# A windowed attention and token mixing kernel: its hand written order of work and its evictions arranged anew

## The chip, the cores and the metric

The kernel runs on one core of a Trainium2 chip. A core has five engines that run side by side, each through its own list of instructions: PE multiplies matrices, DVE and ACT do elementwise work and move results out of PSUM, POOL and SP are used here mainly to issue DMAs. [...] The metric is the device time of one execution in microseconds (us); lower is better.

## The reference

Two layers follow each other. The first is attention with a sliding window of 128 and a linear position bias (8 batches, 8 heads, 576 positions, 64 values per head); the second mixes the tokens of each batch through two small projections.

```python
# attention: q, k, v are [8, 8, 576, 64] in float32
scores = q @ k.T / 8 + bias          # bias = -slope[head] * |i - j|
scores = where((i >= j) & (i - j < 128), scores, -1e9)
attn = softmax(scores)
x = (attn @ v)  -> [8, 576, 512]     # heads side by side
# token mixing, per batch
wq, wk = x @ w_q, x @ w_k            # [576, 64]
W_tok = wq @ wk.T / 8                # [576, 576]
out = relu(W_tok @ x) @ w_out        # [8, 576, 512]
```

W_tok is never formed: the kernel computes G = wk.T x first, and then wq G.

## The kernel before

The work is cut into some 740 named operations, each with one engine. Loops at the end of the kernel create them for every batch b, with what each depends on; they do not set the order. The order is a text, `ORDER`, written out by hand at lines 35 to 117: one word for every operation, such as `QK1.3.0@PE:0`, which says the operation, its engine and the PSUM bank that it fills. Each engine gets its operations in the order in which they stand in the text. An engine never overtakes: an operation that has to wait holds up all that stands behind it on the same engine.

PSUM is held as four pairs of banks, 0 to 3. `:2` takes the whole pair 2, `:20` its first half and `:21` its second. A product can start only when the bank's last content has been moved out.

`+7` behind a bank puts seven zero products ahead of an operation: products of a tile of zeros (`fill`), whose result nobody reads. They keep PE occupied.

The operations of a batch, by name (E in front means the eviction from PSUM):

- `Lq`, `Lk`, `Lv`, `Lt`: loads of 128 rows each of q, k, v, and of the last 64 rows ("tails") of two batches. [...] `Lw`, `Lwo` load the weights. Batch 0 has loads of its own for q and k: `Lf0.0`, `Lf1.0` in float32, issued by SP, and `Lh0.1`, `Lh1.1`, issued by POOL.
- `TQ` and `ETQ`, `TT` and `ETT`: q and k are turned on PE (line 232, for batch 0 also 229), and moved to the tile `qkT` (lines 236 to 244).
- `QKb.g.u`: scores of key block g and half u of the heads; `EXP` (line 551, always ACT): the exponential to the tile `pt`; `MUL` (line 561, always DVE): times the bias and the mask as a factor.
- `PVb.t`: the product with v; `R` (line 612) and `X` (line 615), always DVE: the division by the sum, to the tile `x`. Part 4 is the tails of two batches together.
- `XT`, `EXT`: x turned; `WQ`, `EWQ`: projections to `wqk`; `EWD` (always ACT): a second copy; `WKT`, `EWK` (for the last batch `WK`): k's projection with the tokens in the partitions; `G`, `EG`: the small product to `gs`.
- `MX`, `RM` (lines 755 on ACT, 757 on DVE): the mixed tokens and relu; `OUT`, `EO` (236 on ACT, 238 on DVE): the last product, to the tile `osb`; `DO`: the store, issued by POOL (line 822, tails 825) for the batches 0 to 5, and by SP for 6 and 7. There are 26 buffers `osb` of full width, used in turn.

Before the first batch some constants are made: `iota`, `dist` and `mask` give the distances, `bias0` and `bias1` (ACT) the factors for the two halves of the heads, `biasl0` and `biasl1` copy these for the last key block; `ident` (POOL) and `idh` (DVE) are the identity for turning; `zeros`, `empty`, `ones` (DVE) and `pads` (POOL, three memsets, lines 338 to 340) set columns that no load writes. The distances lie in a part of the tile `nat` that the q rows of batch 3 take later.

Loads on POOL have `iota` ahead of them, and the stores of batches 0 to 5 stand behind all loads. Between two engines the framework adds the waits that follow from tiles; the helpers `apart` and `lone` (lines 248 and 265) take out waits between parts of one bank or tile that do not touch, for operations that hold a bank or write certain tiles, and read the list `deps` for that alone.

## Time and profile before

| | us |
|---|---|
| median of 3 runs | 135.16 |
| lowest, highest | 134.41, 135.35 |
| the profiled execution | 134.84 |
| its span, from the first to the last instruction | 132.8 |

The profile is of one execution. Some rows of it group instructions: a row of the timeline has the start, the length of a group of equal neighbours on an engine, the engine, the line, the operation, what it writes and reads, how many there are (`x4`), and in brackets how long the engine was idle before it and what ended that. A row of the groups has the number of instructions, their busy time, the mean of one in ns, and the idle time before them. PEld is the loading of weights into PE, which goes along with PE. Operations of one kind share a line, so that an operation is found by its place in the order: `ETQ1.0`, say, is the first of the two 2048-wide copies on DVE at line 244.

Most of the work by kind, in the groups of the page:

```profile
L551 ACT ACTIVATE pt<-pair 128x1024 f16<-128x1024 f32 x64 | 63.1, 1040 | 3.6 <-PE pair L229 3.1
L229 PE MATMUL pair<-wout_sb,rm 128*128 128x512 f16 (+1 forms) x132 | 31.9, 373 | 0.2 <-ACT wkn L242 0.2
L561 DVE TENSOR_TENSOR pt<-pt,bias 128x2048 f16<-128x2048 f16 x24 | 29.0, 1216 | 1.6 <-ACT pt L551 1.5
L615 DVE TENSOR_TENSOR x<-pair,inv 128x512 f16<-128x512 f32 x32 | 22.1, 690 | 0.9
```

The exponentials alone are 63.1 us of ACT.

### The profile page before, as it was taken

The page shows a single profiled execution, that of the slowest core. Times are in us where ns is not written, and L with a number is a line of the kernel's source. Part 1 is how long each engine was busy: PE and PEld are TensorE (multiplying, and loading weights), DVE is VectorE, ACT ScalarE, POOL GpSimd, SP SyncE. Part 2 cuts the span into 40 slices and gives each one's busy share as a digit, 9 for nine tenths or more (in the row PEclk, how much of TensorE's full clock was granted, in tenths as well). Part 3 has the DMA queues.
Part 4 walks back from the last instruction along what each step waited for, and adds up shares of the span by engine and source line. Part 5 has one row for each costly group of instructions (what it writes and reads, how often), then busy time and mean ns, then how long its engine had stood idle before and what let it go on. Part 6 is the DMA issues. An engine that isn't in the chain of part 4 may idle for free.

```text
span 132.8 us, 5411 instructions
## 1 busy us (share of the span) xinstructions
PE 119.8 (90%) x2360; PEld 77.9 (59%) x2360; DVE 110.1 (83%) x186; ACT 112.7 (85%) x166; POOL 109.8 (83%) x148
## 2 busy tenths in 40 slices
...
DMA  3999999999999999999999999999999729999963
GB/s 107 261 160 156 155 157 155 155 155 157 181 156 159 154 157 154 154 154 153 155 157 154 156 153 154 154 152 156 153 206 410 300 80 295 352 347 298 352 249 94
DMA packets 111431, 25.12 MB, mean 189 GB/s; under 512 B 105840, under 2 KB 108656, under 8 KB 111408
## 3 DMA queue, kind: packets, MB, share of 16 engines
...
q8 instruction: 18, 0.29, 0.8%
...
## 4 chain that ended last, share of the span: by engine, by line
PE 42%; ACT 26%; DMA 10%; POOL 7%; DVE 6%; issue 5%; POOLq 0%; ACTq 0%; DVEq 0%
PE pair L229 37%; ACT pt L551 15%; DMA nat<-in_k_dram 6%; PE pair L232 5%; DMA vt<-in_v_dram 5%; ACT qkT L242 4%; POOL nat L380 3%; POOL vt L380 3%; DVE pt L561 2%; ACT osb L236 2%; ACT rm L755 2%; ACT wqd L242 1%; DVE x L615 1%; ACT gs L236 1%; DVE wqk L238 1%
## 5 line engine op out<-in xcount | busy, mean ns | idle before, releaser
L551 ACT ACTIVATE pt<-pair 128x1024 f16<-128x1024 f32 x64 | 63.1, 1040 | 3.6 <-PE pair L229 3.1
L380 POOL DMA_DIRECT2D vt<-in_v_dram x32 | 31.4, 1136 | 1.0 <-DMA nat<-in_k_dram 0.8
L229 PE MATMUL pair<-wout_sb,rm 128*128 128x512 f16 (+1 forms) x132 | 31.9, 373 | 0.2 <-ACT wkn L242 0.2
L561 DVE TENSOR_TENSOR pt<-pt,bias 128x2048 f16<-128x2048 f16 x24 | 29.0, 1216 | 1.6 <-ACT pt L551 1.5
L380 POOL DMA_DIRECT2D nat<-in_q_dram x29 | 29.1, 1053 | 0.5 <-ACT wqd L242 0.3
L380 POOL DMA_DIRECT2D nat<-in_k_dram x29 | 28.8, 1051 | 0.1
L229 PE MATMUL pair<-qkT 64*128 64x256 f16 (+2 forms) x320 | 23.0, 250 | 2.0 <-ACT qkT L242 0.8
L229 PEld LDWEIGHTS <-pt 128*128 128x128 f16 (+1 forms) x576 | 18.8, 100 | 7.0 <-issue 2.5
L615 DVE TENSOR_TENSOR x<-pair,inv 128x512 f16<-128x512 f32 x32 | 22.1, 690 | 0.9
L229 PE MATMUL pair<-vt,pt 128*128 128x65 f16 (+1 forms) x512 | 21.6, 194 | 0.9 <-DMA vt<-in_v_dram 0.5
L822 POOL DMA_DIRECT2D out_dram<-osb x24 | 13.6, 628 | 7.5 <-DVE osb L238 5.1
L229 PEld LDWEIGHTS <-rm 128*128 128x128 f16 x132 | 11.4, 97 | 11.2 <-issue 1.2
L236 ACT COPY osb<-pair 128x512 f32<-128x512 f32 (+1 forms) x24 | 13.7, 582 | 3.7 <-PE pair L229 3.7
L229 PEld LDWEIGHTS <-qkT 64*128 64x128 f16 x320 | 11.4, 94 | 8.9 <-issue 3.5
L242 ACT COPY qkT<-pair 128x1024 f32<-128x1024 f32 (+1 forms) x13 | 12.7, 980 | 1.1 <-PE pair L232 1.0
L757 DVE TENSOR_SCALAR rm<-pair 128x1024 f16<-128x1024 f32 (+1 forms) x10 | 11.0, 1113 | 1.6 <-PE pair L229 1.5
L238 DVE COPY osb<-pair 128x512 f32<-128x512 f32 x13 | 8.9, 687 | 4.0 <-PE pair L229 3.9
L229 PE MATMUL pair<-xT,wqk_sb 128*128 128x256 f16 (+1 forms) x64 | 10.1, 286 | 0.6 <-DVE xT L244 0.4
L232 PE MATMUL pair<-identh,nat 64*128 64x64 f16 (+1 forms) x512 | 10.0, 191 | 0.4 <-ACT pt L551 0.2
L232 PEld LDWEIGHTS <-nat 64*128 64x128 f16 (+1 forms) x512 | 9.0, 96 | 1.9 <-issue 1.4
L561 DVE TENSOR_TENSOR pt<-pt,biasl 128x2048 f16<-128x2048 f16 x8 | 9.6, 1205 | 0.0
L612 DVE RECIPROCAL inv<-pair 128x8 f32<-128x8 f32 x36 | 7.3, 202 | 2.6 <-PE pair L229 2.5
...
## 6 DMA issues: line engine op xcount, KB each, us to landing
out_dram<-osb POOLq DMA_DIRECT2D x24, 256.0 KB, 4.7
...
out_dram<-osb SPq DMA_DIRECT2D x7, 256.0 KB, 2.3
...
```

The costliest lines, as they stand in the source:

```text
L229: hold(nc.tensor.matmul(*a, **k))
L232: hold(nc.tensor.transpose(*a))
L236: hold(nc.scalar.copy(out_ap, in_ap))
L238: hold(nc.vector.tensor_copy(out=out_ap, in_=in_ap))
L242: hold(nc.scalar.copy(out_ap.bitcast(FP32), in_ap.bitcast(FP32)))
L380: op = add(kind, b, part, (eng,), deps, lambda o: q.dma_start(out=dst, in_=src), size=size)
L551: nc.scalar.activation(out=pt[:, u, 0:1024], in_=two(s.bank).rearrange("p e c -> p (e c)"), func=AF.Exp, scale=SCALE)
L561: nc.vector.tensor_tensor(out=pt[:, :, 0:1024], in0=pt[:, :, 0:1024], in1=bt, op=ALU.mult)
L612: nc.vector.reciprocal(out=box["inv"], in_=px(64))
L615: nc.vector.tensor_tensor(out=x.rearrange("p (g h d) -> p g h d", g=2, h=4), in0=px(slice(0, 64)), in1=box["inv"].unsqueeze(3).broadcast_t ...
L757: hold(nc.vector.tensor_scalar(out=out_ap, in0=in_ap, scalar1=0.0, scalar2=WSCALE, op0=ALU.max, op1=ALU.mult))
L822: q.dma_start(out=out[b, P * st:P * st + P, c], in_=osb)
```

## The change

The text `ORDER` is replaced by another with the same 737 operations. No operation is added or taken away, and the tiles, shapes and buffers stay. What differs:

- the order on PE, ACT, DVE and POOL. SP keeps its order. On POOL `pads` now comes first; among the loads, `Lt0.0` stands ahead of `Lh1.1`, `Lw1` comes fourth and `Lw0` late, `Lk1.3` is the eleventh load on POOL instead of the eighth, and `Lv1.3` the twenty-first instead of the nineteenth. Among the stores `DO5.3` goes from the eleventh place to the last, and `DO0.1` from the twelfth to the twentieth.
- the PSUM banks of most products.
- the engine of 52 evictions and copies. From DVE to ACT: `ETQ0.0.1.1`, `ETQ0.1.1.1`, `ETQ1.0`, `ETT0`, `ETT4`, `ETT7`, `EXT0.2`, `EXT2.1`, `EXT7.2`, `EWQ1.1`, `EWQ3.0`, `EWQ5.0`, `EWQ7.1`, `EWK2`, `RM0.0`, `RM6.0`, `RM7.3`, `EO0.1`, `EO0.2`, `EO0.3`, `EO2.3`, `EO5.3`, `EO7.0`, `EO7.1`, `EO7.2`. From ACT to DVE: `biasl0`, `ETQ0.1.0.0`, `ETT5`, `EXT0.0`, `EXT1.0`, `EXT1.1`, `EXT4.2`, `EWQ1.0`, `EWQ4.1`, `EWQ6.1`, `EWQ7.0`, `EWK3`, `EWK7.0`, `EWK7.1`, `EWK7.3`, `EG0`, `EG7`, `RM1.1`, `RM1.4`, `RM6.4`, `RM7.1`, `RM7.4`, `EO1.1`, `EO2.0`, `EO5.2`, `EO7.3.0`, `EO7.3.1`.
- the zero products. Before, 21: seven ahead of TQ0.0.0, four ahead of TT0, two each ahead of QK0.0.0 and PV0.2, one each ahead of TQ0.0.1, QK0.0.1, QK0.3.1, TQ1.2, QK1.3.1 and WKT0. After, 29: eight ahead of TQ0.0.0, six ahead of PV0.1, four ahead of QK1.3.0, three ahead of QK0.0.1, two each ahead of QK0.2.0, TQ0.1.1 and QK1.1.0, one each ahead of TQ0.0.1 and TQ1.0.
- the q loads of batch 3 get the two bias operations into their list of dependencies.

```diff
 ORDER = """
-iota@POOL Lf0.0@SP ident@POOL Lf1.0@SP dist@DVE mask@DVE Lh0.1@POOL empty@DVE bias0@ACT Lh1.1@POOL
-zeros@DVE idh@DVE Lt0.1@POOL biasl0@ACT ones@DVE bias1@ACT Lt0.0@POOL TQ0.0.0@PE:0+7 Lq1.2@POOL
-ETQ0.0.0.0@DVE Lk1.2@POOL TQ0.0.1@PE:1+1 Lw0@POOL ETQ0.0.1.0@ACT ETQ0.0.1.1@DVE ETQ0.0.0.1@ACT
-QK0.0.0@PE:2+2 Lk1.3@POOL EXP0.0.0@ACT QK0.1.0@PE:3 TQ0.1.0@PE:1 Lq1.3@POOL EXP0.1.0@ACT TQ0.1.1@PE:0
-QK0.2.0@PE:2 ETQ0.1.1.0@DVE Lv0.0@POOL ETQ0.1.0.0@ACT ETQ0.1.0.1@DVE Lv0.1@POOL QK0.0.1@PE:3+1
-ETQ0.1.1.1@DVE TT0@PE:1+4 EXP0.0.1@ACT Lv0.3@POOL QK0.1.1@PE:0 EXP0.2.0@ACT Lk1.0@POOL MUL0.0@DVE
-QK0.2.1@PE:3 EXP0.1.1@ACT Lv0.2@POOL ETT0@DVE ETT1@DVE QK0.3.1@PE:2+1 Lq1.1@POOL EXP0.2.1@ACT MUL0.1@DVE
-Lq1.0@POOL TQ1.2@PE:0+1 EXP0.3.1@ACT MUL0.2@DVE PV0.0@PE:1 Lk1.1@POOL ETQ1.2@ACT QK0.3.0@PE:3 R0.0@DVE
-biasl1@DVE Lv0.4@POOL EXP0.3.0@ACT QK1.3.1@PE:2+1 X0.0@DVE QK1.3.0@PE:0 Lv1.3@POOL EXP1.3.1@ACT
-MUL0.3@DVE PV0.1@PE:3 Lv1.2@POOL EXP1.3.0@ACT R0.1@DVE Lw1@POOL PV0.2@PE:2+2/10 X0.1@DVE QK1.2.0@PE:1
-R0.2@DVE PV0.3@PE:0 X0.2@DVE EXP1.2.0@ACT Lq2.1@POOL XT0.0@PE:3 R0.3@DVE MUL1.3@DVE QK1.2.1@PE:2
-Lq2.0@POOL EXP1.2.1@ACT TQ1.0@PE:1 X0.3@DVE Lv1.1@POOL EXT0.0@ACT ETQ1.0@DVE XT0.1@PE:2 Lk2.0@POOL
-EXT0.1@ACT PV0.4@PE:0 Lk2.1@POOL QK1.1.0@PE:1 R0.4@DVE QK1.0.0@PE:3 X0.4@DVE EXP1.1.0@ACT QK1.1.1@PE:2
...
-G7.0@PE:00 EWK7.3@ACT DO4.0@POOL G7.1@PE G7.2@PE RM6.1@DVE G7.3@PE EWD7@ACT OUT6.1@PE:01 EG7@ACT
-DO5.4@POOL MX7.3@PE:2 MX7.1@PE:3 MX7.2@PE:1 RM7.3@DVE RM7.1@ACT OUT6.0@PE:00 EO6.1@ACT RM7.2@DVE
-OUT7.3.1@PE:30 EO6.0@DVE DO6.1@SP OUT6.2@PE:01 EO7.3.1@ACT DO6.0@SP OUT6.3@PE:31 EO6.2@ACT DO7.3.1@SP
-DO6.2@SP OUT7.3.0@PE:30 EO6.3@ACT OUT7.1@PE:00 EO7.3.0@ACT DO6.3@SP MX6.4@PE:2 DO7.3.0@SP MX7.0@PE:1
-EO7.1@DVE MX7.4@PE:3 OUT7.2@PE:01 RM7.0@ACT DO7.1@SP RM7.4@ACT RM6.4@ACT OUT7.0@PE:10 EO7.2@DVE
-OUT7.4@PE:11 DO7.2@SP EO7.0@DVE DO7.0@SP EO7.4@ACT DO7.4@SP
+pads@POOL Lf0.0@SP empty@DVE iota@POOL Lf1.0@SP zeros@DVE ident@POOL ones@DVE dist@DVE Lh0.1@POOL
+mask@DVE Lt0.0@POOL bias1@ACT Lh1.1@POOL bias0@ACT biasl1@DVE TQ0.0.0@PE:0+8 Lw1@POOL idh@DVE
+ETQ0.0.0.1@ACT ETQ0.0.0.0@DVE Lt0.1@POOL TQ0.0.1@PE:1+1 biasl0@DVE Lk1.2@POOL ETQ0.0.1.1@ACT Lq1.3@POOL
+ETQ0.0.1.0@ACT QK0.2.0@PE:2+2 EXP0.2.0@ACT Lv0.1@POOL QK0.0.0@PE:3 QK0.1.0@PE:0 TQ0.1.0@PE:1 Lv0.0@POOL
+EXP0.1.0@ACT ETQ0.1.0.0@DVE ETQ0.1.0.1@DVE Lq1.2@POOL EXP0.0.0@ACT TQ0.1.1@PE:2+2 ETQ0.1.1.0@DVE
+Lk1.3@POOL ETQ0.1.1.1@ACT QK0.0.1@PE:0+3 QK0.1.1@PE:1 Lq1.1@POOL EXP0.0.1@ACT QK0.2.1@PE:3 TT0@PE:2
+Lv0.2@POOL ETT0@ACT ETT1@DVE EXP0.1.1@ACT MUL0.0@DVE QK0.3.0@PE:0 QK0.3.1@PE:2 Lq1.0@POOL EXP0.2.1@ACT
+MUL0.1@DVE Lk1.0@POOL EXP0.3.0@ACT Lv0.3@POOL MUL0.2@DVE PV0.1@PE:1+6 EXP0.3.1@ACT Lk1.1@POOL R0.1@DVE
+TQ1.2@PE:3 X0.1@DVE Lk2.1@POOL ETQ1.2@ACT MUL0.3@DVE Lv1.2@POOL QK1.3.0@PE:0+4 QK1.3.1@PE:2 Lv0.4@POOL
+EXP1.3.0@ACT QK1.2.1@PE:1 PV0.2@PE:3 Lv1.3@POOL EXP1.3.1@ACT R0.2@DVE PV0.0@PE:0 X0.2@DVE Lq2.0@POOL
+EXP1.2.1@ACT R0.0@DVE QK1.2.0@PE:2 MUL1.3@DVE Lq2.1@POOL EXP1.2.0@ACT TQ1.0@PE:3+1 Lk2.0@POOL PV0.3@PE:1
+ETQ1.0@ACT R0.3@DVE Lv1.1@POOL X0.0@DVE QK1.1.0@PE:2+2 X0.3@DVE QK1.0.1@PE:3 Lv1.0@POOL EXP1.1.0@ACT
+XT0.0@PE:0 MUL1.2@DVE QK1.1.1@PE:1 Lw0@POOL EXP1.0.1@ACT PV0.4@PE:2 EXT0.0@DVE EXP1.1.1@ACT QK1.0.0@PE:3
+Lq2.3@POOL R0.4@DVE X0.4@DVE EXP1.0.0@ACT MUL1.1@DVE Lk2.3@POOL XT0.2@PE:20 XT0.1@PE:0 EXT0.1@ACT
+TQ2.0@PE:1 Lq2.2@POOL MUL1.0@DVE PV1.3@PE:3 ETQ2.0@ACT Lk2.2@POOL PV1.2@PE:0 R1.3@DVE EXT0.2@ACT
+R1.2@DVE PV1.1@PE:1 Lt2.0@POOL X1.2@DVE WQ0.1@PE:21 R1.1@DVE Lwo0@POOL X1.3@DVE WQ0.0@PE:20 EWQ0.1@ACT
+Lt2.1@POOL X1.1@DVE EWQ0.0@ACT XT1.1@PE:0 QK2.0.0@PE:3 EXT1.1@DVE EWD0@ACT QK2.0.1@PE:2 Lwo1@POOL
+WKT0@PE:10 EXP2.0.0@ACT XT1.2@PE:11 Lwo3@POOL EXT1.2@DVE PV1.0@PE:0 WQ1.1@PE:11 Lwo2@POOL R1.0@DVE
+EXP2.0.1@ACT EWK0@DVE X1.0@DVE G0@PE:10 Lq3.2@POOL EWQ1.1@ACT XT1.0@PE:3 EG0@DVE Lk3.3@POOL TQ2.2@PE:0
+EXT1.0@DVE MX0.1@PE:2 ETQ2.2@ACT MX0.0@PE:1 Lk3.2@POOL RM0.1@DVE WQ1.0@PE:30 RM0.0@ACT Lq3.1@POOL
+MX0.4@PE:0 EWQ1.0@DVE QK2.2.1@PE:2 RM0.4@DVE Lq3.3@POOL EWD1@ACT WKT1@PE:31 TT2@PE:1 EXP2.2.1@ACT
...
+RM6.1@DVE EWK7.2@ACT G7.0@PE:10 EWQ7.1@ACT G7.1@PE G7.2@PE G7.3@PE EWD7@ACT OUT6.1@PE:00 EG7@DVE
+MX7.2@PE:2 EO6.1@ACT MX7.3@PE:3 MX7.1@PE:1 RM7.2@DVE OUT6.0@PE:01 RM7.3@ACT DO6.1@SP OUT7.3.1@PE:00
+EO6.0@DVE OUT6.2@PE:30 EO7.3.1@DVE DO6.0@SP RM7.1@DVE OUT6.3@PE:31 DO7.3.1@SP EO6.2@ACT DO6.2@SP
+MX7.0@PE:2 EO6.3@ACT MX6.4@PE:0 MX7.4@PE:1 OUT7.3.0@PE:30 RM7.0@ACT DO6.3@SP OUT7.1@PE:31 EO7.3.0@DVE
+RM7.4@DVE DO7.3.0@SP OUT7.2@PE:30 RM6.4@DVE EO7.1@ACT DO7.1@SP OUT7.0@PE:31 EO7.2@ACT DO7.2@SP
+OUT7.4@PE:30 EO7.0@ACT DO7.0@SP EO7.4@ACT DO7.4@SP
 """
...
-                    loads[b, j, n] = load("L" + "qk"[j], b, n, ("c", 1024, 256), [tq.get((b - NNAT, j, n)), *([tq[0, j, 2 * b - 4]] if b in (2, 3) else [])],
+                    loads[b, j, n] = load("L" + "qk"[j], b, n, ("c", 1024, 256), [tq.get((b - NNAT, j, n)), *([tq[0, j, 2 * b - 4]] if b in (2, 3) else []), *(mkb if b == 3 and j == 0 else [])],
```

## The prediction

> **What bounds the kernel now.** First the page, for the share of each engine and the slices, then the windows, for the stretches in which the engines are full and those in which they wait.

> ```profile
> span 132.8 us, 5411 instructions
> PE 119.8 (90%) x2360; PEld 77.9 (59%) x2360; DVE 110.1 (83%) x186; ACT 112.7 (85%) x166; POOL 109.8 (83%) x148
> ...
> DMA  3999999999999999999999999999999729999963
> ...
> 9.00:25.00 16.00, 12.47 (x330) 8.19 (x331) 13.24 (x21) 14.02 (x17) 14.84 (x18) 1.00 2.42 156
> 25.00:38.40 13.40, 11.58 (x256) 8.24 (x249) 11.58 (x20) 10.88 (x16) 13.09 (x20) 1.00 2.16 162
> 38.40:103.50 65.10, 63.92 (x1305) 42.15 (x1298) 62.21 (x104) 64.11 (x86) 62.98 (x77) 1.00 2.32 173
> 103.50:119.20 15.70, 15.59 (x282) 11.00 (x283) 13.41 (x26) 12.66 (x26) 10.22 (x19) 1.00 0.77 268
> 119.20:132.80 13.60, 8.93 (x66) 4.27 (x64) 5.01 (x7) 5.41 (x12) 0.56 (x2) 0.99 0.73 251
> ```

> A window row gives its length, then the busy time of PE, PEld, DVE, ACT and POOL, the granted clock, and the DMA figures. From 38.4 to 103.5 ACT works 64.11 of 65.10 us, PE 63.92, DVE 62.21, and POOL, which issues the loads, is hardly ever free: four engines are full, so no new order can take much out of this half of the run. What waiting there is, a better order could remove only before 38.4 (ACT idle 1.98 us from 9 to 25, and 2.52 us from 25 to 38.4) and after 103.5. The clock is granted in full throughout, and the DMA engines are full from the second slice to the thirtieth, so the moment at which a load lands is set by its place in the stream of loads. The waits at the start, ACT's rows first, then those of the other engines:

> ```profile
> 9.03 1.94 ACT L551 ACTIVATE pt<-pair 128x1024 f16<-128x1024 f32 x2
> 11.93 1.94 ACT L551 ACTIVATE pt<-pair 128x1024 f16<-128x1024 f32 x2 [0.48 <-PE pair L229]
> ...
> 17.08 1.03 ACT L242 COPY qkT<-pair 128x1024 f32<-128x1024 f32 x1
> ...
> 22.52 1.02 ACT L551 ACTIVATE pt<-pair 128x1024 f16<-128x1024 f32 x1 [0.29 <-PE pair L229]
> ...
> 26.40 3.77 ACT L551 ACTIVATE pt<-pair 128x1024 f16<-128x1024 f32 x4 [1.60 <-PE pair L229]
> ...
> 31.63 1.02 ACT L242 COPY qkT<-pair 128x1024 f32<-128x1024 f32 x1 [0.87 <-PE pair L232]
> ...
> 38.44 2.85 ACT L551 ACTIVATE pt<-pair 128x1024 f16<-128x1024 f32 x3
> ...
> 1.64 0.90 POOL L380 DMA_DIRECT2D nat<-in_q_dram  x1
> ...
> 9.97 0.33 PEld L232 LDWEIGHTS <-nat 64*64 64x64 f16 x32 [0.23 <-DMA nat<-in_k_dram]
> 10.21 2.63 POOL L380 DMA_DIRECT2D vt<-in_v_dram  x3 [0.84 <-DMA nat<-in_k_dram]
> ...
> 15.74 0.64 PE L232 MATMUL pair<-identh,nat 64*128 64x64 f16 x32
> ...
> 23.70 1.22 DVE L244 COPY qkT<-pair 128x2048 f16<-128x2048 f16 x1
> ...
> 24.57 0.19 PE L229 MATMUL pair<-vt,pt 128*64 128x65 f16 x1 [0.25 <-DMA vt<-in_v_dram]
> ...
> 25.19 0.18 POOL L338 MEMSET wqk<- 128x64 f16 x1
> 25.36 0.34 POOL L340 MEMSET xT<- 128x256 f16 x1
> ...
> 26.08 0.44 PEld L229 LDWEIGHTS <-qkT 64*128 64x128 f16 x9 [0.80 <-issue]
> ```

> Read them so: the first exponential is at 9.03; ACT's largest wait, 1.60 us, ends at 26.40 with QK1.1.0. That product stood behind ETQ1.0, the 1.22 us eviction on DVE, behind PV0.4, whose last load (Lv1.3, the 19th that POOL issues) let it go on at 24.57, and behind 0.80 us of "issue", which no wait explains. The exponentials of the full stretch begin at 38.44.

> **The change, part by part.** *Waits and instructions.* The edit at line 414 adds the bias evictions to what Lq3.* depends on. A load holds no bank, so both helpers that read this list return before using it, and the list gives no instruction: 0. If it did, Lq3.2 would wait for an activation done before 9.03, some 25 us earlier.

> *Pads to the front of POOL.* Three memsets, 25.19 to 25.70, 0.51 us, now precede iota, identity and the first load (1.64 to 2.15). Covered: TQ0.0.0 reads a load issued on SP, and the DMA engines are full from the second slice on. In the middle POOL gets back the 0.42 us between 25.19 and its next load. Uncovered, it would cost 0.51. I take 0 for the start, and keep -0.4 to +0.5 for the stream.

> *Zero products, 21 to 29.* Price by rows:

> ```profile
> 1.19 3.17 PE L229 MATMUL pair<-fill 128*128 128x512 f16 x7 [1.19 <-DVE fill L360]
> ...
> 11.85 1.02 PE L229 MATMUL pair<-fill 128*128 128x512 f16 x4
> ```

> At the start one takes (3.17-0.63)/6 = 0.42 us, later (1.02-0.39)/3 = 0.21. The eighth before TQ0.0.0 ends at about 4.8, where that product began at 4.70: +0.1, lost again because ACT is now only ready at 9.0 through three evictions (below). The six before PV0.1 take 1.3 us from the end of EXP0.1.1 (about 14.8); PV0.1 waits for MUL0.1 to about 16.1 anyway (1.2 us on DVE, as the copy of equal size at 23.70). The four before QK1.3.0 fill the time of ETQ1.2. All lie in PE's 3.5 idle us of 9 to 25: cost 0, and if each set were 0.1 to 0.2 late, +0.5.

> *The first exponentials.* ETQ0.0.1.1 goes to ACT, so three of the four evictions stand there, done about 9.02 as before; EXP0.2.0, 0.1.0, 0.0.0 follow to 11.87. Lh1.1 (PE got it at 9.97) is now issued behind Lt0.0, one place later: 9.97 + 0.87 = 10.8 (2.63 us for three issues at 10.21: 0.87 a place). TQ0.1.1 0.5 us, its eviction on DVE 0.7, QK0.0.1 at 12.1: EXP0.0.1 at 12.5, against 11.93, but with one exponential more before it instead of a copy: even by 13.9.

> *TQ1.2 waits longer.* Its last load was the ninth, now it is the eleventh (Lk1.3): two places, 1.74 us, so TQ1.2 moves from 15.7 (its row at 15.74) to 17.4. ETQ1.2 comes at 18.2 instead of 17.08; EXP0.3.0 and 0.3.1 stand before it, and end at 17.55: 0.6 us idle, then 0.45 until QK1.3.0 has run. By EXP1.2.0, which ends about 23.45 (before, the row at 22.52 ended at 23.54), this is paid by the gaps of 0.48, 0.33 and 0.29 that go, and ETT0 is done besides: 0.

> *ETQ1.0 to ACT.* 1.03 us directly behind, to 24.5. DVE is free of 1.22; QK1.1.0 can run at 24.6 and EXP1.1.0 at 24.95, 1.45 before the old 26.40. What is late next: PV0.4, now behind QK1.1.0. Lv1.3 is the 21st load, 24.57 + 1.74 = 26.3; QK1.0.0 stands behind PV0.4 on PE and is ready at 27.7, when ACT has just done three exponentials (24.95 + 2.85 = 27.8). So it fits, with nothing to spare. The four end at 28.75, against 30.17.

> *From there to the full stretch.* PV1.3, PV1.2 and PV1.1 now stand ahead of WQ0.1 and WQ0.0, and PV1.1 needs MUL1.0 (30.6 at the earliest: EXP1.0.0 ends 28.75, MUL1.1 before it). WQ0.1 thus runs at 31.3 and its eviction at 32.0, after ETQ2.0 and EXT0.2 left ACT idle at 30.85: 1.15 us given back. EXP2.0.0 about 33.5 (33.35 before), then EXP2.0.1, EWQ1.1, ETQ2.2, RM0.0, EWD1. The exponentials of the full stretch start at 38.5, against 38.44, with RM0.0 already done. Head in all: +0.1.

> *The evictions exchanged.* 25 go to ACT, 27 to DVE. The prices:

> ```profile
> L236 ACT COPY osb<-pair 128x512 f32<-128x512 f32 x22 | 13.0, 601 | 3.2 <-PE pair L229 3.2
> L242 ACT COPY qkT<-pair 128x1024 f32<-128x1024 f32 x12 | 12.4, 1031 | 1.1 <-PE pair L232 1.0
> L757 DVE TENSOR_SCALAR rm<-pair 128x1024 f16<-128x1024 f32 x8 | 9.8, 1220 | 1.3 <-PE pair L229 1.2
> L238 DVE COPY osb<-pair 128x512 f32<-128x512 f32 x13 | 8.9, 687 | 4.0 <-PE pair L229 3.9
> L755 ACT ACTIVATE rm<-pair 128x1024 f16<-128x1024 f32 x6 | 6.3, 1042 | 0.7 <-PE pair L229 0.7
> L242 ACT COPY xT<-pair 128x512 f32<-128x512 f32 x7 | 4.1, 585 | 0.3 <-PE pair L232 0.2
> ```

> What counts is what runs from 38.4 to 103.5. To ACT: EO0.1, 0.2, 0.3 and 2.3, 4 x 0.60 = 2.40; EXT2.1 0.59. To DVE: EO1.1 and 2.0, 1.20; RM1.1 1.04. The small ones (RM1.4, ETT, EWK, EWQ, EXT4.2; 0.2 to 0.5 us each) come to nearly nothing as they go both ways. ACT +0.75, DVE 0.8 to 0.9 less. ACT's instructions overlap a little (three exponentials take 2.85, each 1.04: 0.91 apart), so +0.65. ACT's 0.99 idle us there could take all of it or none: 0 to 0.65; I take 0.4, nearer the upper end since ACT is the fuller of the two.

> *The tail.* The products and their order up to RM7.* are nearly the same: MUL7.0 now precedes EXT6.1 on DVE, which EXP7.2.* take up, and EG7 stands behind RM6.1 on DVE; by their durations each is worth at most 0.2, in opposite directions. At the end:

> ```profile
> out_dram<-osb POOLq DMA_DIRECT2D x24, 256.0 KB, 4.7
> ...
> 107.72 2.14 POOL L822 DMA_DIRECT2D out_dram<-osb  x4 [5.08 <-DVE osb L238]
> ...
> 121.09 0.58 ACT L236 COPY osb<-pair 128x512 f32<-128x512 f32 x1
> ...
> 125.02 0.28 PEld L229 LDWEIGHTS <-gs 64*128 64x128 f16 x12 [0.42 <-issue]
> ...
> 128.16 0.59 ACT L236 COPY osb<-pair 128x512 f32<-128x512 f32 x1 [1.60 <-PE pair L229]
> ```

> MX7.0, MX6.4 and MX7.4, at 125.02 now directly ahead of OUT7.2, move ahead of OUT7.3.0, so that three products cover their evictions: -0.3. The last four full products share two half banks, each freed by a 0.6 us copy: +0.1. Tail -0.2. On POOL the stores are reordered; DO5.3, for which POOL stood 5.08 us, goes to the end, so the queue is done sooner, which nobody waits for except a buffer of the 26: EO6.1 (121.09) reuses that of EO0.1, whose store is now the twentieth, behind DO5.1: issued about 113, landed 4.7 later, 3 us to spare.

> **Sum.** +0.1 +0.4 -0.2 = +0.3. The profiled execution took 134.84 us, span 132.8 and 2.0 around it; 134.84 + 0.3 = 135.1, which is the median of 135.16.

> [...] Chance 0.03.

> **The rivals.** *Faster, 0.20.* The "issue" stall at 26.08 does not return and the 1.45 us won at EXP1.1.0 reach the full stretch, because X and PV of batch 1 run earlier than I laid them. Bound: there TQ and PV wait for loads at POOL's fixed pace; with the 0.42 of the pads and an equal slack (an estimate from the 0.25 wait at 24.57) some 0.8 get through. With -0.2 to -0.6 in the tail and nothing for the evictions: 134.84 - 1.3 = 133.5. Against it: ACT has more work, not less.

> *Slower, 0.22.* One mechanism: loads late at PV0.4. If Lv1.3 lands after about 26.3, everything behind PV0.4 on PE (QK1.0.0, XT0.2, TQ2.0, PV1.*) shifts by the same, and ACT, 98% full afterwards, cannot catch up. It decides as soon as the delay exceeds 0.1; two more places (1.74) cost some 1.4, and with 0.65 for the evictions in full and the tail as above: 134.84 + 1.9 = 136.7. For it: PE stood at that very load before, at place 19.

> *No change, 0.55:* the sum above; by itself 134.2 to 136.1.

> **How the numbers follow.** A measurement tells about 1% (1.35 us) from no change. Faster by more holds most of the first rival, slower most of the second: 0.21, 0.55, 0.24. The range of 8 in 10 reaches to both rivals' times: 133.6 to 136.7. "Issue" stalls of up to 0.8 us can turn up at another product and are in it on both sides.

> **What would show it.** Right: first exponential at 9.0; ETQ1.2 later, about 18; no wait above 0.6 before EXP1.1.0, at about 25; ACT idle about 1 us near 31; exponentials of batch 2 (the run after RM0.0) from 38.5; ACT 0.5 busier and DVE 0.8 less in a stretch like 38.4 to 103.5; POOL's stores done by 116. Wrong: EXP1.1.0 after 26, or PE waiting for vt over 0.5 us; the stretch starting a microsecond sooner or later; PE idle over 0.5 us at the last three MX.

## The result, and the profile after

| | before | after |
|---|---|---|
| median, us (21 runs each) | 135.16 | 135.76 |
| lowest, highest | 134.27, 137.61 | 135.04, 137.04 |
| ratio after to before, 95% interval | | 1.0067 [1.0043, 1.0091] |
| measured again (a1_same below), us | 134.88 (24 runs) | 135.93 (10 runs) |
| its ratio | | 1.0074 [1.0046, 1.0102] |

The forecast was 135.1 us, no change. The time lies in the range given, but the kernel became slower by about 0.7%, and both intervals lie above 1. Medians are of all executions, while the ratios, here and below, leave out those in a slower state (six of the 21 before, of 136.85 us and more; five of twelve of b2_v13_late, one of six of b3_engines_there, four of 13 of b4_no_w). The other 15 before have a median of 134.81 us, so the difference is about 0.9 us. The profiled execution of the changed kernel was its slowest, 137.04 us, so two more executions of the same kernel were profiled: 135.69 us (called the second profile) and 134.78 us (the third).

The clock row of the page of the changed kernel, first profile, and then that of the third:

```profile
PEclk9999959999999999999999999999999999999999
```

```profile
PEclk9999999999999999999999999999999999999996
```

In the first, one slice in the head is granted half the clock. The two windows around it (length, then busy time of PE, PEld, DVE, ACT, POOL, then the granted clock):

```profile
12.92:16.33 3.41, 1.75 (x41) 1.41 (x42) 0.93 (x2) 2.24 (x4) 2.77 (x4) 1.00 2.43 154
16.33:19.74 3.41, 3.39 (x22) 1.74 (x21) 2.90 (x3) 2.72 (x3) 3.27 (x5) 0.50 2.44 157
```

PE worked 1.75 of 3.41 us, and in the next 3.41 us its clock was 0.50. What it stood for is in PE's timeline of the same execution:

```profile
5.31 1.50 PE L229 MATMUL pair<-ident,nat 64*64 64x64 f32 x64 [0.52 <-DMA nat<-in_q_dram]
...
12.41 0.39 PE L229 MATMUL pair<-qkT 64*128 64x256 f16 x3 [0.25 <-DVE qkT L238]
13.77 0.72 PE L229 MATMUL pair<-qkT 64*128 64x256 f16 x9 [0.97 <-issue]
...
15.43 0.85 PE L229 MATMUL pair<-qkT 64*128 64x192 f16 x16 [0.71 <-ACT qkT L242]
16.35 2.72 PE L229 MATMUL pair<-fill 128*128 128x512 f16 x6
```

QK0.0.1 has four products. Three ran at 12.41, then PE stood 0.97 us for nothing but "issue", and the fourth ran at 13.77. In the kernel before, the wait of this kind ended at the same moment, but stood ahead of TT0. It was not free there either: QK0.1.1 stands right behind TT0, and ACT stood 0.49 us for it ahead of EXP0.1.1. The rows of the kernel before, PE and then ACT:

```profile
13.69 0.41 PE L232 MATMUL pair<-identh,natt 64*128 64x64 f16 x16 [0.82 <-issue]
...
13.93 0.60 PE L229 MATMUL pair<-qkT 64*128 64x256 f16 x8
...
14.35 2.85 ACT L551 ACTIVATE pt<-pair 128x1024 f16<-128x1024 f32 x3 [0.49 <-PE pair L229]
```

In the changed kernel ACT stands 1.39 us ahead of EXP0.0.1 in the first profile, and 0.79 and 0.76 in the other two. In the first, the six zero products then took 2.72 us at half the clock (1.45 in the third). ACT's rows of the third profile, the quickest execution of the changed kernel, which answer to ACT's rows in the prediction:

```profile
8.87 2.86 ACT L551 ACTIVATE pt<-pair 128x1024 f16<-128x1024 f32 x3
...
12.97 1.02 ACT L551 ACTIVATE pt<-pair 128x1024 f16<-128x1024 f32 x1 [0.76 <-PE pair L229]
...
18.28 1.01 ACT L242 COPY qkT<-pair 128x1024 f32<-128x1024 f32 x1 [0.34 <-PE pair L232]
...
24.95 3.77 ACT L551 ACTIVATE pt<-pair 128x1024 f16<-128x1024 f32 x4 [0.49 <-PE pair L229]
...
31.49 0.81 ACT L236 CAST wqk<-pair 128x320 f16<-128x320 f32 x2 [1.21 <-PE pair L229]
...
38.12 2.86 ACT L551 ACTIVATE pt<-pair 128x1024 f16<-128x1024 f32 x3
...
102.96 0.39 ACT L236 CAST gs<-pair 128x256 f16<-128x256 f32 x1
...
128.18 0.59 ACT L236 COPY osb<-pair 128x512 f32<-128x512 f32 x1 [0.28 <-PE pair L229]
```

Set beside the same points of the kernel before (its EG5 is the row below, the others stand in the prediction) and of the other two profiles, this says where the time went. All in us from the start of the span; "to" is the distance from the point above.

```profile
103.18 0.37 ACT L236 CAST gs<-pair 128x256 f16<-128x256 f32 x1
```

| point | before | after, first | second | third |
|---|---|---|---|---|
| first exponential | 9.03 | 9.36 | 8.87 | 8.87 |
| EXP0.0.1, the first of the second half of the heads | 11.93 | 14.09 | 12.99 | 12.97 |
| EXP1.1.0 | 26.40 | 27.20 | 24.98 | 24.95 |
| start of the full stretch of exponentials | 38.44 | 40.36 | 39.01 | 38.12 |
| end of EG5 | 103.55 | 105.61 | 104.27 | 103.35 |
| to: middle | 65.11 | 65.25 | 65.26 | 65.23 |
| end of the last eviction | 128.75 | 131.00 | 129.67 | 128.77 |
| to: tail | 25.20 | 25.39 | 25.40 | 25.42 |

The middle is 0.12 to 0.15 longer and the tail 0.19 to 0.22 in all three. The rest, from -0.3 to +1.9 us, is made in the first 38 us and differs from one execution to the next. Of the 2.24 us by which the first profile is behind the third at the full stretch, half (1.12) is there at EXP0.0.1, and the other half has come up by EXP1.1.0, over the stretch at half the clock. The window of the third profile over the full stretch used in the prediction:

```profile
38.40:103.50 65.10, 63.60 (x1284) 40.73 (x1286) 61.20 (x100) 64.01 (x87) 63.84 (x79) 1.00 2.31 172
```

DVE is 1.0 us less busy there than before (61.20 against 62.21), ACT as full as it was (64.01 against 64.11).

### The profile page after: what moved, and what is told of

It is laid out like the page before. It is cut to its first block, busy times and chain, and to the rows that moved or that the text cites. A ratio compares the mean times of both kernels' runs of the same rounds, so it can differ in the third digit from the quotient of the medians.

```text
span 135.0 us, 5437 instructions
## 1 busy us (share of the span) xinstructions
PE 121.9 (90%) x2368; PEld 77.2 (57%) x2368; DVE 107.4 (80%) x189; ACT 113.1 (84%) x163; POOL 109.8 (81%) x148
## 3 DMA queue, kind: packets, MB, share of 16 engines
q1 hardware_dynamic: 2512, 3.41, 7.5%
## 4 chain that ended last, share of the span: by engine, by line
PE 55%; ACT 26%; DVE 8%; issue 4%; DMA 3%; ACTq 0%; DVEq 0%
PE pair L229 48%; ACT pt L551 17%; PE pair L232 7%; ACT qkT L242 4%; DMA nat<-in_q_dram 3%; DVE pt L561 3%; ACT osb L236 2%; DVE qkT L238 1%; ACT rm L755 1%; DVE x L615 1%; DVE rm L757 1%; ACT qkT L236 1%; DVE gs L238 1%; ACT wqk L236 1%; DVE osb L238 1%
## 5 line engine op out<-in xcount | busy, mean ns | idle before, releaser
L551 ACT ACTIVATE pt<-pair 128x1024 f16<-128x1024 f32 x64 | 63.1, 1046 | 3.3 <-PE pair L229 3.0
L229 PE MATMUL pair<-wout_sb,rm 128*128 128x512 f16 (+1 forms) x132 | 32.1, 374 | 0.0
L380 POOL DMA_DIRECT2D vt<-in_v_dram x32 | 31.8, 1124 | 0.0
L380 POOL DMA_DIRECT2D nat<-in_q_dram x29 | 29.9, 1054 | 1.7 <-ACT wqk L236 1.1
L380 POOL DMA_DIRECT2D nat<-in_k_dram x29 | 29.5, 1058 | 0.1
L229 PE MATMUL pair<-qkT 64*128 64x256 f16 (+2 forms) x320 | 23.0, 250 | 3.9 <-ACT qkT L242 1.0
L229 PEld LDWEIGHTS <-pt 128*128 128x128 f16 (+1 forms) x576 | 19.2, 101 | 7.0 <-issue 2.9
L229 PE MATMUL pair<-vt,pt 128*128 128x65 f16 (+1 forms) x512 | 21.6, 195 | 1.1 <-ACT pt L551 0.6
L615 DVE TENSOR_TENSOR x<-pair,inv 128x512 f16<-128x512 f32 x32 | 21.6, 684 | 0.9 <-DVE inv L612 0.2
L236 ACT COPY osb<-pair 128x512 f32<-128x512 f32 x27 | 16.2, 606 | 6.1 <-PE pair L229 6.0
L822 POOL DMA_DIRECT2D out_dram<-osb x24 | 13.5, 589 | 6.6 <-ACT osb L236 4.9
L229 PEld LDWEIGHTS <-qkT 64*128 64x128 f16 x320 | 11.6, 94 | 11.8 <-issue 4.6
L229 PEld LDWEIGHTS <-rm 128*128 128x128 f16 x132 | 11.2, 97 | 11.6 <-issue 1.9
L242 ACT COPY qkT<-pair 128x1024 f32<-128x1024 f32 (+1 forms) x16 | 14.7, 919 | 2.3 <-PE pair L232 2.0
L229 PE MATMUL pair<-fill 128*128 128x512 f16 x29 | 10.7, 501 | 1.3 <-DVE fill L360 1.2
L757 DVE TENSOR_SCALAR rm<-pair 128x1024 f16<-128x1024 f32 (+1 forms) x9 | 9.9, 1100 | 1.3 <-PE pair L229 1.3
L232 PE MATMUL pair<-identh,nat 64*128 64x64 f16 (+1 forms) x512 | 10.0, 191 | 0.5 <-ACT pt L551 0.5
L229 PE MATMUL pair<-xT,wqk_sb 128*128 128x320 f16 (+1 forms) x64 | 10.0, 286 | 0.0
L232 PEld LDWEIGHTS <-nat 64*128 64x128 f16 (+1 forms) x512 | 8.5, 96 | 1.9 <-issue 1.7
## 6 DMA issues: line engine op xcount, KB each, us to landing
out_dram<-osb POOLq DMA_DIRECT2D x24, 256.0 KB, 4.3
out_dram<-osb SPq DMA_DIRECT2D x7, 256.0 KB, 2.0
```

The costliest lines, as they stand in the source:

```text
L229: hold(nc.tensor.matmul(*a, **k))
L232: hold(nc.tensor.transpose(*a))
L236: hold(nc.scalar.copy(out_ap, in_ap))
L242: hold(nc.scalar.copy(out_ap.bitcast(FP32), in_ap.bitcast(FP32)))
L380: op = add(kind, b, part, (eng,), deps, lambda o: q.dma_start(out=dst, in_=src), size=size)
L551: nc.scalar.activation(out=pt[:, u, 0:1024], in_=two(s.bank).rearrange("p e c -> p (e c)"), func=AF.Exp, scale=SCALE)
```

## The experiments

The theories: (1) the head is slower through the "issue" stall inside QK0.0.1; (2) the loss is in the evictions of the middle; (3) the load Lv1.3, now later, paces the head; (4) the tail; (5) the clock; (6) the whole stream of loads. Ratios are to the kernel before on the same chip, which took 134.7 to 134.9 us in every group. Edits are shown as the words that differ, with the rest of their lines left out.

### The same kernel again

> The changed kernel once more, for a second profile. The first profile was of its slowest execution, 137.04 us, with a half clock from 16.3 to 19.7. Theory 1 (the loss is in the head: PE stands 0.97 us of issue inside QK0.0.1, at the 447th PE instruction of the trace, and ACT 1.39 us with it): the stall stands there again and ends near 13.7, the first exponential of half 1 comes at about 14.1, EXP1.1.0 at about 26 to 27, and from there the shift against before stays nearly the same to the end. Theory 2 (the loss is in the middle, where ACT got more evictions): the run of exponentials starts near 38.5 as forecast, and the stretch behind it is 0.4 to 0.65 us longer than the 65.1 of before. Time 135.6 to 135.9 by both.

Median 135.93 us, 1.0074 [1.0046, 1.0102]. The stall stands in QK0.0.1 again, but ends at 12.68, a microsecond sooner than in the first profile. What is late instead, from the timeline (PE, DVE and ACT rows):

```profile
27.12 0.19 PE L229 MATMUL pair<-vt,pt 128*64 128x65 f16 x1 [0.88 <-DMA vt<-in_v_dram]
...
27.90 0.21 DVE L612 RECIPROCAL inv<-pair 128x8 f32<-128x8 f32 x1 [1.02 <-ACT pt L551]
28.15 0.69 DVE L615 TENSOR_TENSOR xtl<-pair,inv 128x512 f16<-128x512 f32 x1
...
28.75 2.35 DVE L561 TENSOR_TENSOR pt<-pt,bias 128x2048 f16<-128x2048 f16 x2
...
32.40 0.81 ACT L236 CAST wqk<-pair 128x320 f16<-128x320 f32 x2 [1.21 <-PE pair L229]
```

PV0.4 stands 0.88 us for Lv1.3, which in this execution landed 0.9 us later than in the third (27.08 against 26.17). Behind PV0.4 stand R0.4 and X0.4 on DVE (27.90, 28.15; the profile names ACT as their releaser, but its exponential was long done), behind these MUL1.1 and MUL1.0, and PV1.1, WQ0.1 and EWQ0.1 wait for the last. From EXP1.1.0, level with the third profile, the second is 0.9 later at the full stretch and stays so to the end.

> The changed kernel for a third look. Theory 6: an execution of 135.3 to 136 us with no stretch at half clock shows a load that landed 0.3 to 1 us later than in the quickest traces (Lv1.3 at 26.0, Lv1.0 at 30.3, Lv3.2 at 58.3), and PE waiting for just that one; the rest of the run is shifted by that much. If the loads lie where they were and the time is up all the same, the cause is another.

134.78 us, the third profile: no late load, no half clock, the stall short (0.35 us). So this expectation was not met as written: it was made for an execution of 135.3 to 136 us. It shows what the changed order does undisturbed: it ends where the profile before ends (128.77 and 128.75). But the profile before is of an ordinary execution. Quickest against quickest, the changed kernel stays behind by 0.8 us in the first measurement (135.04 and 134.27) and by 0.5 in the second (134.94 and 134.43).

### The evictions of the middle

```diff
-EO0.1@ACT EO0.2@ACT EO0.3@ACT EO2.3@ACT EXT2.1@ACT EO1.1@DVE EO2.0@DVE RM1.1@DVE
+EO0.1@DVE EO0.2@DVE EO0.3@DVE EO2.3@DVE EXT2.1@DVE EO1.1@ACT EO2.0@ACT RM1.1@ACT
```

> The changed kernel with the engines of eight evictions of the middle as they were before: EO0.1, EO0.2, EO0.3, EO2.3 and EXT2.1 back to DVE, EO1.1, EO2.0 and RM1.1 back to ACT; the order stays. Theory 2: the time falls by 0.4 to 0.65 us against a1_same, to about 135.2. Theory 1: the same time as a1_same within 0.2, since the middle cost only about 0.1 in the traces.

Median 137.53 us, 1.0198 [1.0168, 1.0227]: not 0.4 faster than the changed kernel but 1.6 us slower. The place, in the timeline:

```profile
46.27 1.22 DVE L757 TENSOR_SCALAR rm<-pair 128x1024 f16<-128x1024 f32 x1
...
47.40 0.68 DVE L238 COPY osb<-pair 128x512 f32<-128x512 f32 x1
...
48.13 1.02 PE L229 MATMUL pair<-wout_sb,rm 128*128 128x512 f16 x4 [1.12 <-DVE osb L238]
...
49.20 0.59 ACT L236 COPY osb<-pair 128x512 f32<-128x512 f32 x1 [1.79 <-PE pair L229]
```

EO0.2 stands on DVE behind RM1.0. OUT1.2 needs its half bank and waits 1.12 us, and ACT 1.79 for OUT1.2.

> The kernel before with the engines of the eight evictions of the middle as the change has them (EO0.1, EO0.2, EO0.3, EO2.3 and EXT2.1 on ACT, EO1.1, EO2.0 and RM1.1 on DVE), its order kept. Theory 2 as the prediction had it: ACT, the fullest engine, pays 0.4 to 0.65 us, 135.3 to 135.5. Against it stands that the reverse exchange in the changed kernel cost 1.5 us: if each order is only fit for its own engines, this one loses more than 1 us as well, 136 or more, and the exchange and the order have to be judged as one.

Median 136.66 us, or 136.55 of the five in the ratio, 1.0116 [1.0086, 1.0146]: the reverse exchange in the order before costs 1.7 us as well. In both profiles the loss is in the middle, which is 67.47 us long in a3_engines_back (65.2 in the changed kernel) and 66.97 here (65.11 in the kernel before). Theory 2 falls, and with it the way the evictions were priced: an order is fit for its own engines. That an eviction's cost is who stands behind it, not the fullness of the engine, is what the rows of a3_engines_back show; for the reverse exchange no row here shows it.

### The stall

The index of an instruction counts PE's weight loads and products together, in the trace. In 16 of the 20 traces PE stalls so for 0.3 us or more in the head, each time ahead of the 447th: TT0's first in the kernel before (0.82 us), QK0.0.1's fourth product in the changed one (0.97, 0.37 and 0.35 in its three profiles), which has 16 zero products ahead of it and not 11. The second one of the kernel before (26.08 in the prediction, 0.52 us for PE) is ahead of the 959th, 512 further on.

```diff
-TQ0.0.0@PE:0+8 TQ0.0.1@PE:1+1 QK0.2.0@PE:2+2 TQ0.1.1@PE:2+2 QK0.0.1@PE:0+3
+TQ0.0.0@PE:0+7 TQ0.0.1@PE:1 QK0.2.0@PE:2 TQ0.1.1@PE:2 QK0.0.1@PE:0
```

> Nine zero products fewer ahead of QK0.2.1 (the sets ahead of TQ0.0.1, QK0.2.0, TQ0.1.1 and QK0.0.1 and one of those ahead of TQ0.0.0), so that the 447th PE instruction falls on TT0 as it did before. Theory 1: PE stands at TT0 and no longer at QK0.0.1, EXP0.0.1 starts at about 12.9 instead of 14.1, but ETT0 stands on ACT ahead of EXP0.1.1 and comes at 14.4, so that 0.6 us stay; time 0.3 to 0.8 below a1_same, about 135.2. Theory 2 (evictions in the middle) and theory 3 (loads pace the head): the same time as a1_same within 0.2. If the zero products do what they are named for and keep the clock, the granted clock falls to half in the head and the time rises above a1_same.

Median 135.64 us, 1.0057 [1.0036, 1.0078], 0.3 below the changed kernel on the same chip, which the intervals do not separate. EXP0.0.1 did start at 12.35, without a wait. The gain is lost behind it: PV0.4 (0.34 us) and PV1.1 (0.26) wait for loads. And in 11 of its 12 executions the mean clock was below 0.99, against 5 of 10 of the changed kernel on the same chip and 2 of 21 in the first measurement: nine zero products fewer went with a lower clock here. So this run does not price the stall by itself.

```diff
-QK0.0.1@PE:3+1 ... TT0@PE:1+4
+QK0.0.1@PE:3+6 ... TT0@PE:1
```

> The kernel before, with the four zero products ahead of TT0 moved to QK0.0.1 and one more, so that six stand there and the 447th PE instruction is the fourth product of QK0.0.1, as in the changed kernel; nothing else. Theory 1: PE stands inside QK0.0.1 until about 13.7, EXP0.0.1 starts at 14.0 instead of 11.93, EXP1.1.0 at about 27 instead of 26.40, and the time rises by 0.5 to 1.2 us, to about 136. If the stall is not bound to the count of PE instructions, or the loads take the delay up (theory 3), the time stays within 0.3 of 135.2.

Median 135.38 us, 1.0041 [1.0019, 1.0063], so 0.5 us slower with nothing but zero products moved in the kernel before. PE's rows:

```profile
12.62 0.39 PE L229 MATMUL pair<-qkT 64*128 64x256 f16 x3
13.70 0.28 PE L229 MATMUL pair<-qkT 64*128 64x256 f16 x1 [0.69 <-issue]
```

The stall is inside QK0.0.1, at the fourth product, as the count said, and EXP0.0.1 starts at 14.0 instead of 11.93. In 8 of its 9 executions the mean clock was below 0.99, the profiled one among them, so the 0.5 us may hold some half clock too; the one execution at full clock took 135.25 us, 0.4 above the kernel before. That is far less than the 2.1 us by which EXP0.0.1 is late: the order before has room behind it.

The price of the stall in the changed order can be read across the traces, since its end moves by itself. In ten traces with it on QK0.0.1, EXP0.0.1 starts 0.32 us after it, at 12.94 to 14.09, 13.41 in the mean. In three traces in which neither a load nor the clock disturbs the head, the span follows it one to one (in a7_more_zero and a9_no_w, which have other edits, the difference is 120.0 and 120.1):

| kernel | EXP0.0.1 | span | difference |
|---|---|---|---|
| third profile | 12.97 | 132.8 | 119.8 |
| a4_v13_early | 13.46 | 133.3 | 119.8 |
| a6_pads_back | 13.73 | 133.5 | 119.8 |

When the stall ends goes with the very first products. In the third profile TQ0.0.0 took 1.16 us from 4.72, to 5.88, and the stall ended at 12.65; in a9_no_w it took 1.82 to 6.54, and the stall ended at 13.43; in the first it started late, at 5.31, took 1.50 to 6.81, and the stall ended at 13.77 (PE rows of the three timelines).

### The loads

```diff
-Lk1.1@POOL Lk2.1@POOL Lv1.2@POOL Lv0.4@POOL Lv1.3@POOL Lq2.0@POOL Lq2.1@POOL
+Lk1.1@POOL Lv1.3@POOL Lv1.2@POOL Lv0.4@POOL Lk2.1@POOL Lq2.0@POOL Lq2.1@POOL
```

> The changed kernel with the loads Lv1.3 and Lk2.1 exchanged: Lv1.3 is issued eighteenth on POOL, at about 17.4 instead of 20.0, and Lk2.1, which TQ2.0 needs at about 29, in its place. Theory 3 (the head is paced by the load Lv1.3: PV0.4 stands 0.88 us for it in the second profile, and behind it in the order of DVE R0.4, X0.4, MUL1.1, MUL1.0, and so PV1.1, WQ0.1 and ACT's wait of 1.21 us): PV0.4 runs at 26.1 to 26.3 without a wait for vt, EWQ0.1 starts near 31.6 instead of 32.4, and the median falls by 0.5 to 0.9 us to 134.9 to 135.3. If the head is paced by something else (theory 1, the issue stall; or the next loads Lv1.1 and Lv1.0), the time is that of a1_same within 0.3.

Median 135.35 us, 1.0047 [1.0021, 1.0072]. PV0.4 no longer waits for a load, EWQ0.1 starts at 31.98, and the median is just above the 134.9 to 135.3 expected; the interval overlaps that of the changed kernel, so a gain is not shown for certain.

```diff
-Lv1.3@POOL Lq2.0@POOL Lq2.1@POOL
+Lq2.0@POOL Lq2.1@POOL Lv1.3@POOL
```

> The changed kernel with Lv1.3 two places later still, behind Lq2.0 and Lq2.1, which move up. Theory 3: its load lands at 27.8 instead of 26.0 to 27.1, PV0.4 waits for it by 1.6 us, and everything behind comes 0.8 to 1.7 us later; median 136.6 to 137.5. If the load is not what paces the head: within 0.4 of a1_same.

Median 136.98 us, 1.0144 [1.0108, 1.0180]: 1.0 to 1.2 us above the changed kernel, and in the expected range. A late load has a price, but not all of this is the wait: in the profile PV0.4 went on at 27.79 as expected, after a wait of 0.59 us and not of 1.6, and four of the six executions had a mean clock of 0.987 or less.

The kernel before, with Lv1.3 at the place of the change:

```diff
-Lv0.4@POOL Lv1.3@POOL Lv1.2@POOL Lw1@POOL
+Lv0.4@POOL Lv1.2@POOL Lw1@POOL Lv1.3@POOL
```

> The kernel before with Lv1.3 at the twenty-first place, where the change has it (Lv1.2 and Lw1 move up one), and nothing else. Theory 3: it lands at 26.1 instead of 24.5 and PE stands there 1.6 us; some 0.8 us of that are taken out of the issue stall that QK1.1.0 has in the kernel before, so EXP1.1.0 comes at 27.1 instead of 26.40 and the time rises by 0.7 to 1.5 us, to 135.6 to 136.4. If loads do not pace the head, 134.9 to 135.2 as before.

Median 137.34 us, or 136.59 of the seven in the ratio, 1.0129 [1.0086, 1.0172], more than expected. PE's wait is the expected one, but in the window with most of it PE works only 1.62 of 3.41 us, and the next two windows have half the clock (0.51 and 0.50):

```profile
25.84 0.19 PE L229 MATMUL pair<-vt,pt 128*64 128x65 f16 x1 [1.66 <-DMA vt<-in_v_dram]
```

```profile
23.28:26.69 3.41, 1.62 (x54) 1.33 (x55) 1.63 (x3) 1.15 (x3) 3.41 (x7) 1.00 2.43 152
26.69:30.10 3.41, 3.03 (x26) 1.67 (x21) 2.58 (x5) 3.23 (x4) 3.41 (x5) 0.51 2.42 155
```

Its two executions at full clock took 135.38 and 135.52 us, the ten others 136.41 and more.

The memsets at the front of POOL:

```diff
-pads@POOL Lf0.0@SP empty@DVE iota@POOL
+Lf0.0@SP empty@DVE iota@POOL
...
-Lv1.0@POOL EXP1.1.0@ACT
+Lv1.0@POOL pads@POOL EXP1.1.0@ACT
```

> The changed kernel with the three memsets of pads taken from the front of POOL and put behind Lv1.0. If the 0.4 us at the front delay the whole stream of loads and the loads pace the head, every load to Lv1.0 lands 0.4 us sooner and the time falls by 0.3 to 0.5 us, to 135.4. If the stream is set by the DMA engines and not by POOL's issues, as the prediction had it at cost 0, the landings stay and the time is that of a1_same within 0.2.

Median 136.32 us, 1.0099 [1.0065, 1.0132], not faster. Seven of its twelve executions had a mean clock of 0.987 or less and took 136.32 to 136.96; the five others took 135.09 to 135.93, like the changed kernel. That the pads cost something is not shown.

The six weights left out of the stream, in either kernel; in the order their six words go from POOL to DVE, behind mask (changed kernel) or idh (before):

```diff
     def load(kind, b, part, size, deps, dst, src, eng="POOL"):
+        if kind[:2] == "Lw":
+            return add(kind, b, part, DVE, [], lambda o: nc.vector.memset(dst, 0.0), size=size)
```

> The changed kernel with the six loads of the weights (Lw0, Lw1, Lwo0 to Lwo3) left out of POOL's stream: their tiles are set to zero on DVE behind mask, so the output is zero. POOL's stream is about 3.7 us shorter by PV3.3 (two issues of 0.75 and four of 0.55). Theory 6 (after the change the kernel runs at the pace of the stream of loads: in the traces PV0.4, PV1.2, TQ2.0, PV1.1, PV3.3 and TQ5.2 start at most 0.35 us after their last load has landed, where the kernel before had 0.6 to 2.6 us at most of them, so a load that lands late goes straight into the time): with the stream ahead these gaps grow to 1 us and more, the time falls by 0.7 to 1.2 us to 134.3 to 134.8 and the runs lie closer together. If the changed order itself is slow (theories 2 and 4), the time stays at 135.5 to 135.9.

> The kernel before with the same six loads left out and their tiles set to zero on DVE behind idh; the output is zero. Theory 6: it has room at most loads, so it gains less than the changed kernel, 0.0 to 0.5 us, 134.4 to 134.9. If both gain alike, the stream paces both, and the difference between them has another cause.

The opposite came out for the changed kernel: it took 135.87 us, 1.0066 [1.0037, 1.0095], the same as with its loads. The kernel before gained about what was expected of it: 134.38 us, or 134.18 of the nine in the ratio, 0.9951 [0.9924, 0.9979]. Every load of the changed kernel had room now, and the stall was what was left (code lines are one less in this kernel):

```profile
13.43 0.72 PE L228 MATMUL pair<-qkT 64*128 64x256 f16 x9 [0.90 <-issue]
```

Theory 6 falls as the one cause. Loads and stall are two limits of the head that lie close together: with the loads gone the stall sets the pace, with the stall gone (a2_fewer_zero) the loads do, as far as one trace of each can show it.

### The clock

```diff
-QK0.3.0@PE:0 ... XT0.2@PE:20 ... QK1.1.0@PE:2+2
+QK0.3.0@PE:0+2 ... XT0.2@PE:20+2/00 ... QK1.1.0@PE:2+3
```

> The changed kernel with five more zero products in PE's waits of the head: two ahead of QK0.3.0, two ahead of XT0.2, one ahead of QK1.1.0. Theory 5 (the clock): in the ten traces so far, every stretch of 3.41 us in which PE was busy for 0.51 or less of it, and none in which it was busy for 0.62 or more, was followed by one at half the clock; the change puts two waits of 0.97 and 0.70 close together near 13 to 15 and a wait for Lv1.3 near 26, and where such a stretch happens to fall on them the run takes 1 to 2 us more. With more zero products hardly a run shows a mean clock of 0.987 or less (seven of twelve did in a6, five of ten in a1_same), and the median falls to about 135.4, lowest as before near 135.0. If the clock is not the cause of the upper half of the runs, the median stays at 135.8 to 136.0.

Median 135.60 us, 1.0058 [1.0035, 1.0081]. None of its six executions had a mean clock below 0.992, and none took more than 135.80. The upper end is gone, but the median is only 0.2 to 0.3 lower: the clock makes the slowest executions, not the middle ones. Its quickest execution, 134.93 us, is no faster than the third profile. The first measurement says the same of the clock: 19 of its 21 executions of the changed kernel had a mean clock of 0.99 or more, and their median is 135.58 us.

### Mending

> The changed kernel with the causes found so far mended together: Lv1.3 and Lk2.1 exchanged (theory 3); one zero product less ahead of QK0.0.1, so that all four of its products stand before the 447th PE instruction, and EXP0.1.1 ahead of ETT0 on ACT and MUL0.0 ahead of ETT1 on DVE, which the stall would hold up (theory 1); three zero products ahead of QK0.3.0 and two ahead of XT0.2 (theory 5); in the tail MUL7.0 behind EXT6.2, so that EXP7.2.0 does not wait for XT6.1's bank (0.60 us of idle ACT there now). Theory 1 and 3: EXP0.0.1 at 12.4, EWQ0.1 at 31.4 to 31.8, and the stretch from the end of EG5 to the end of EO7.4 25.2 us instead of 25.40; median 134.4 to 134.9, level with before or 0.3 below it. If only the load counts: 135.2 as in a4_v13_early, less 0.2 in the tail.

The edits are those named there. Median 135.61 us, 1.0058 [1.0031, 1.0084], not the 134.4 to 134.9 expected. EXP0.0.1 did start at 12.35. But in the middle PV3.3 now stood for a load, and in the tail ACT's wait ahead of EXP7.2.0 stayed, though MUL7.0 was out of the way:

```profile
58.91 0.64 PE L229 MATMUL pair<-vt,pt 128*128 128x65 f16 x16 [0.40 <-DMA vt<-in_v_dram]
```

```profile
109.70 1.94 ACT L551 ACTIVATE pt<-pair 128x1024 f16<-128x1024 f32 x2 [0.62 <-PE pair L229]
```

In the third profile the same wait is 0.61. So EXT6.1 behind MUL7.0 is not its cause. PE's rows there show OUT5.2 and, without idle time behind it, QK7.2.1 and QK7.2.0: ACT waits because PE itself is busy.

```profile
108.08 1.04 PE L229 MATMUL pair<-wout_sb,rm 128*128 128x512 f16 x4
109.05 0.61 PE L229 MATMUL pair<-qkT 64*128 64x256 f16 x8
```

The tail, in which MUL7.0's new place is the only edit, became 0.4 us longer.

> The changed kernel with its head mended alone: Lv1.3 and Lk2.1 exchanged, Lw1 (first used near 31 us) taken from the fourth place of POOL's stream to behind Lv1.0, one zero product less ahead of QK0.0.1, EXP0.1.1 ahead of ETT0 and MUL0.0 ahead of ETT1, zero products as in a8_mended; the tail as in the change. Theory 6: up to Lv1.0 the loads land 0.7 us sooner, ETQ2.2 starts at 35.2 to 35.5 (36.57 in a1_same), but by the middle the stream is where it was, PV3.3 or TQ5.2 waits for its load there, and the end stays where a7_more_zero had it: median 134.9 to 135.4. If the middle is not paced by the stream, the head's gain reaches the end: 134.2 to 134.7.

Median 135.30 us, 1.0046 [1.0020, 1.0072]. ETQ2.2 started at 36.2, not at 35.2 to 35.5: EXP0.0.1 came at 12.7, but EXP0.1.1 stood for the stalled products to 14.11, and ETQ1.2 0.65 us for TQ1.2. What the middle would do with a gain was not tested, as there was none.

> The changed kernel with three things at once: only seven zero products ahead of QK0.2.1 (five ahead of TQ0.0.0, two ahead of QK0.2.0), so that the 447th PE instruction is past QK0.0.1, QK0.1.1 and QK0.2.1; EXP0.1.1 and MUL0.0 ahead of ETT0 and ETT1; and room for the loads (Lv1.3 and Lk2.1 exchanged, Lw1 behind Lv1.0). Zero products instead ahead of QK0.3.0 and XT0.2. Theory 1: in eleven traces of the changed order with the stall on QK0.0.1 the start of EXP0.0.1 is the end of the stall plus 0.32, anywhere from 12.9 to 14.1, and where nothing else is late the end comes 115.8 after it; without the stall EXP0.0.1 starts at 12.3 to 12.6 in every run and the end comes 0.5 to 1 us sooner: median 134.3 to 134.8, below a13_stall_on by 0.5 to 1.0, with less spread. If fewer zero products bring the half clock back, it shows as a mean clock below 0.99 and takes the gain.

> The same kernel as a12_stall_off with the zero products ahead of QK0.2.1 as in the change (eight, one, two, two, three), so that the 447th PE instruction is again the fourth product of QK0.0.1: its control. Theory 1: EXP0.0.1 at 12.9 to 14.0, median 135.0 to 135.5. If it is level with a12_stall_off within 0.3, the stall is not what costs the time.

135.35 us, 1.0036 [1.0017, 1.0055], and 135.36 us, 1.0042 [1.0017, 1.0066]: level (in these two and the next, PV0.1 has four zero products instead of six). The pair does not decide. With five zero products at the start, TQ0.0.0 and TQ0.0.1 together took 3.59 us, the first exponential came at 9.46, and EXP0.0.1 at 12.94 all the same. In the control, a new wait of these edits' own making shows (Lw1 ahead of Lw0 made Lw0 late): WQ0.1 stood 0.65 us for it.

> a12_stall_off with all eight zero products kept ahead of TQ0.0.0 and one ahead of QK0.2.0 (nine ahead of QK0.2.1, so that the 447th PE instruction is its second or third product, behind QK0.0.1 and QK0.1.1). In the trace of a12_stall_off the full clock came only at 8.1 us, TQ0.0.0 took 1.82 us instead of 1.05 and the first exponential started at 9.45 instead of 8.87, which ate the 0.6 us that the stall gave back. Theory 1: with the early clock kept, EXP0.0.1 starts at 12.3 to 12.4, ETQ2.2 at 35.0 to 35.3, and the median is 134.3 to 134.9. If the time stays at 135.3 and EXP0.0.1 does start at 12.4, something behind it in the head (loads, DVE) sets the pace, and the stall is not worth its length.

135.46 us, 1.0046 [1.0020, 1.0072]. The stall is off: EXP0.0.1 at 12.54, EXP1.1.0 at 24.39, 0.56 sooner than in the third profile. It does not reach EWQ0.1, which starts at 31.62, later than there:

```profile
30.05 0.64 PE L229 MATMUL pair<-vt,pt 128*128 128x65 f16 x16 [0.24 <-DMA vt<-in_v_dram]
30.89 1.14 PE L229 MATMUL pair<-xT,wqk_sb 128*128 128x320 f16 x8 [0.20 <-DMA wqk_sb<-in_moe_w_q_dram]
31.62 0.81 ACT L236 CAST wqk<-pair 128x320 f16<-128x320 f32 x2 [1.77 <-PE pair L229]
```

PV1.1 waits for Lv1.0 and WQ0.1 for Lw0. The time saved at the stall is waited out at the loads. No version tried that has all its loads beats the kernel before. One with the stall off the first exponentials and more room at the loads as well, without the late Lw0 and with the tail left alone, was not tried.

## Why the prediction was wrong, step by step

- **Waits, pads.** Ahead of Lq3.2 POOL has one wait, before and after, so the edit at line 414 added none there, as said. The pads cost nothing that could be shown (a6_pads_back).
- **The zero products: the step that failed, with the load ahead of PV0.4.** "All lie in PE's 3.5 idle us of 9 to 25: cost 0." They do lie in idle time, but each also moves PE's count of instructions on, and the wait of 0.8 us that cost ACT 0.49 us behind TT0 came to lie inside QK0.0.1, where ACT stood 0.76, 0.79 and 1.39 us. The prediction knew "issue" stalls that "can turn up at another product" and left their place open, on both sides. It could have been counted: 16 zero products and not 11 stand ahead of QK0.0.1. What this is worth by itself is shown for the order before alone (b1_zero_moved, 0.4 to 0.5 us). In the changed order the stall taken off QK0.0.1 brought 0.3 to 0.4 us at most, within the intervals (a2_fewer_zero, a14_stall_off_early), since loads then waited.
- **The first exponentials.** Forecast 9.0 for the first, found 8.87 to 9.36. EXP0.0.1 was put at 12.5 and came at 12.97, 12.99 and 14.09, 13.41 in the mean of ten traces. This delay, 0.5 us in a quiet execution and 0.9 in the mean, is not in the sum.
- **TQ1.2 and ETQ1.0.** The times are right where nothing disturbs: ETQ1.2 at 18.28 after 0.34 idle (forecast 18.2, 0.6), EXP1.1.0 at 24.95 (forecast 24.95). For TQ1.2 that is in part luck. Its load, which was to set it, had landed at 17.27 in the third profile; TQ1.2 ran at 17.60, behind PV0.1, which stood for MUL0.1 to 17.04 and not to 16.1.
- **PV0.4.** "It fits, with nothing to spare" was right, and nothing to spare was the trouble: PE did not stand for the load in the third profile and stood 0.88 us for it in the second, and all of that reached the end. The slower rival's mechanism is real, with a price of 0.9 us in the second profile and 1.0 to 1.2 for two places more (a5_v13_late, some half clock included); it strikes some executions and not all. The prediction weighed it as yes or no.
- **To the full stretch.** ACT's idle time at EWQ0.1 was 1.21 us (forecast 1.15), and the stretch began at 38.12 undisturbed (forecast 38.5). So the head's sum was, if anything, too high for a quiet execution and too low for an ordinary one. The faster rival failed as argued: the 1.45 us won at EXP1.1.0 are given back at EWQ0.1.
- **The evictions.** Forecast +0.4 us, found +0.12 to +0.15. DVE fell by 1.0 (forecast 0.8), ACT did not become 0.5 busier in that stretch. The exchange alone, tried both ways, is worth 1.6 to 1.7 us in favour of the engines that fit the order, a size the pricing by busy time could not give.
- **The tail.** Forecast -0.2, found +0.2. The three products moved ahead of OUT7.3.0 did not cover anything: in the kernel before and after, the last evictions follow PE's products, and their order among themselves does not make PE's work less (from 119.2 to 132.8 it is busy 8.94 us in the third profile, and 8.93 before). From the end of EG5 to EXP7.2.0 the third profile takes 5.90 us against 5.64 before, which is all of the 0.2: there ACT stands 0.61 us for PE, where the forecast allowed 0.2 in opposite directions. POOL's stores ended at 118.3 in the third profile and at 120.6 in the first, not 116, and nobody waited for them.
- **POOL's issues beside the copies on DVE.** The chance of 0.03 was the author's estimate for loads that POOL issues late while biasl0 is copied on DVE. No run shows such a delay. In the kernel before, the two issues around the copy of biasl1 (17.80, 0.76 us) are 0.82 apart, at 17.38 and 18.20. In the second profile POOL's issues stay 0.86 us apart while biasl0 is copied (7.69) and are 0.99 apart where biasl1 is (6.24), against the prediction's 0.87 a place: 0.1 us at most.

For the quickest execution the sum is -0.3 for the head, +0.1 for the middle and +0.2 for the tail: 0.0. For an ordinary one, the second profile, it is +0.6, +0.15 and +0.2: 0.9, which is the difference that was measured, against +0.1, +0.4 and -0.2 in the forecast. So the head was put 0.5 too low and the tail 0.4, and the middle 0.25 too high, which hid part of it. The head's part comes in ways that the runs show one by one: the stall on the path (0.4 in the mean over the quickest), a load that lands late (0.9 when it does), and, in the slowest executions, half the clock (about 1 us when it falls into the head). How often each strikes was not counted, and that they add up to the difference of the medians is argued, not shown: no run of the changed order took all of them away. The prediction also took 1% as the least change that a measurement tells from none; the intervals here reach 0.3% to either side, so that 0.7% shows.
